# A dynamic convolution and a two-layer feed-forward block: 64-row matmul tiles in pairs, 1024-token superblocks, and one x tile with shifted views

## The chip, the cores and the metric

The kernel runs on one core of a Trainium2 chip. Times are microseconds (us) of device time for one execution. A median is given with its lowest and highest run. A ratio is computed as the mean time of one kernel's fast runs over the mean time of the other's in the same rounds, so it is not quite the ratio of the medians that are quoted; its 95% interval stands in brackets. "Fast" is the undisturbed state of an execution. Runs that were made only once have no known state, and this text says so where it uses one.

Engines in the profile: PE is the tensor engine (PEld its weight loads), DVE the vector engine, ACT the scalar engine, POOL is GpSimd, SP the engine whose queue issues most of the transfers. "L124" is line 124 of the kernel in question.

## The reference

For every token and each of 8 heads, a softmax over 7 weights is taken, and the token's 24 channels of that head become the weighted sum of the token itself and its six predecessors. The result, 192 channels, goes through two matrices with `h - tanh(h)` between them.

```python
# x: (8, 4096, 192); weight_gen: (8, 4096, 8, 7); w_in: (192, 2048); w_out: (2048, 192)
w = np.exp(weight_gen - max);  w = w / (sum(w) + 1e-09)
x_unf = x_pad[:, idx, :]                       # seven shifted copies of x, zeros before the start
conv = np.einsum('bshk,bskhg->bshg', w, x_unf) # (8, 4096, 192)
h = conv.reshape(32768, 192) @ w_in
out = (h - np.tanh(h)) @ w_out                 # (32768, 192)
```

## The kernel before

It works through 64 superblocks of 512 tokens. A partition holds every 128th token, so each of the seven taps is its own load of x (seven times the bytes). GpSimd multiplies each tap by its weights, the vector engine adds the taps in pairs, and PE transposes and adds the four sums by matmuls with the identity. 192 channels are split into 128 and 64, the second part padded to 128 rows.

```python
        for k in range(K):                      # seven loads of x
            xs_k = xpool.tile([P, NB, D], FP32, name=f"xs{k}", tag=f"xs{k}")
            ...
        for k in range(K):
            prod = ppool.tile([P, NB, DP], BF16, name=f"prod{k}", tag=f"prod{k}")
            nc.gpsimd.tensor_mul(
                prod[:, :, 0:D].rearrange("p j (h g) -> p j h g", h=H),
                xs[k][:].rearrange("p j (h g) -> p j h g", h=H),
                wsm[:, :, :, k : k + 1].to_broadcast([P, NB, H, G]),
            )
        ...
                    nc.vector.tensor_add(       # pairs of taps
                        acc[:, :, 0:D], prods[taps[0]][:, :, 0:D], prods[taps[1]][:, :, 0:D]
                    )
        ...
            for g in range(NG):                 # transposition and sum, 4 x 128 columns
                nc.tensor.matmul(
                    pc[:, 0:P], lhsT=gsums[g][:, j0, 0:D0], rhs=ident[:],
                    start=st0, stop=False,
                )
        ...
            nc.tensor.matmul(ph[:, 0:TOK], lhsT=w_in0[:, fa * P : (fa + 1) * P],
                             rhs=convT[:], start=True, stop=False)
            ...
            nc.scalar.activation(out=th[:], in_=ph[:], func=ACT.Tanh)
            nc.vector.tensor_sub(gt[:], ph[:], th[:])
```

(Arguments are folded onto fewer lines here, comments are added, and parts are left out at the "..." lines.) The order of the parts on each engine comes from the framework's scheduler, with pools of two to four buffers deciding what may run ahead.

The softmax here doesn't subtract the row's maximum and nothing guards it: scores larger than these inputs give would overflow.

## Time and profile before

| | before |
|---|---|
| median of 3 runs (lowest to highest) | 1046.02 us (1043.23 to 1046.31) |
| span of the profiled run, granted PE clock | 1041.2 us, 0.987 |
| busy: PE, DVE, ACT, POOL | 89%, 77%, 64%, 71% |
| bytes moved by the DMA queues | 211.48 MB |

The "busy" line of the page gives, for each engine, the microseconds in which it worked, the share of the span, and the number of instructions. A group line gives line, engine, operation and shapes, then busy time and the mean duration in ns of one, then the idle time ahead of them with what ended most of it. A line of the waits reads: engine and line, "<-" what it waited for, then total us, how many times, and the longest. In short: PE is close to its rate through the middle of the kernel, and the other engines have 23% to 36% of their time to spare.

### The profile page before, as it was taken

How to read it: one execution, taken by the hardware profiler on the slowest of the kernel's cores; microseconds unless marked ns; L12 is line 12 of the kernel's file. 1: busy time of each engine (PE TensorE's matmuls, PEld its weight loads, DVE VectorE, ACT ScalarE, POOL GpSimd, SP SyncE). 2: the span in 40 equal slices, each digit the busy share in tenths (PEclk: the TensorE clock that was granted, in tenths of full speed). 3: DMA queues.
4: the chain of work that ended last, by engine and by line, in shares of the span. 5: the costliest groups of instructions: out<-in, count | busy, mean ns of one | idle time of the engine just before them, and what ended most of it. 6: DMA issues, size and time to landing. Idle time of an engine off the chain costs nothing.

```text
span 1041.2 us, 20956 instructions
## 1 busy us (share of the span) xinstructions
PE 931.3 (89%) x8192; PEld 661.6 (64%) x8192; DVE 803.0 (77%) x945; ACT 665.2 (64%) x961; POOL 739.3 (71%) x713
## 2 busy tenths in 40 slices
PE   0576777798999999999999999999999999999998
PEld 0344554465666777667776777667776777777776
DVE  1587777797887888788887888788887888877665
ACT  0254445465666777767776777677776777777775
POOL 4868868898786778867787778867787777882000
PEclk9999899899999999999999999999999999999999
DMA  8947588687997787777776777777876777510001
GB/s 167 314 132 230 169 242 250 202 264 223 331 289 208 236 242 222 220 214 235 238 219 205 236 237 233 216 211 231 243 223 202 235 227 239 153 62 27 21 31 47
DMA packets 306579, 211.48 MB, mean 203 GB/s; under 512 B 44312, under 2 KB 306288, under 8 KB 306480
## 3 DMA queue, kind: packets, MB, share of 16 engines
q1 hardware_dynamic: 304192, 208.58, 67.4%
q0 software_dynamic: 2288, 1.57, 1.1%
q8 instruction: 64, 1.05, 0.4%
q14 instruction: 35, 0.29, 0.1%
HBM read 186.52 MB, written 25.17 MB: 203 GB/s over the span
## 4 chain that ended last, share of the span: by engine, by line
PE 55%; POOL 17%; DVE 9%; issue 5%; ACT 5%; SPq 4%; DMA 3%; POOLq 0%; ACTq 0%; DVEq 0%
POOL prod L155 17%; PE po L272 10%; PE po L279 10%; PE ph L248 8%; PE ph L227 7%; PE ph L234 7%; PE ph L241 7%; DVE gt L258 5%; PE pc L194 2%; DVE gsum L174 2%; DMA wg_t<-in_weight_gen_dram 2%; SPq L123 2%; PE pc L206 2%; PE pc L198 2%; PE pc L202 2%
## 5 line engine op out<-in xcount | busy, mean ns | idle before, releaser
L155 POOL TENSOR_TENSOR prod<-xs,wsm 128x768 bf16<-128x768 f32 x448 | 687.1, 1563 | 100.1 <-DVE wsm L146 45.5
L256 ACT ACTIVATE th<-ph 128x1024 f32<-128x1024 f32 x512 | 519.1, 1023 | 283.9 <-PE ph L248 270.9
L258 DVE TENSOR_TENSOR gt<-ph,th 128x1024 bf16<-128x1024 f32 x512 | 609.9, 1210 | 83.0 <-ACT th L256 82.4
L272 PE MATMUL po<-w_out_t,gt 128*128 128x192 bf16 x2048 | 383.4, 248 | 2.1 <-ACT out_sb L288 2.1
L279 PE MATMUL po<-w_out_t,gt 128*128 128x192 bf16 x2048 | 383.1, 248 | 0.0
L227 PE MATMUL ph<-convT,w_in 128*128 128x512 bf16 x512 | 196.6, 384 | 57.0 <-DVE gt L258 55.5
L279 PEld LDWEIGHTS <-gt 128*128 128x128 bf16 x2048 | 201.8, 99 | 27.2 <-issue 4.8
L272 PEld LDWEIGHTS <-gt 128*128 128x128 bf16 x2048 | 201.9, 99 | 24.7 <-issue 1.3
L248 PE MATMUL ph<-convT,w_in 128*128 128x512 bf16 x512 | 197.1, 385 | 0.0
L241 PE MATMUL ph<-convT,w_in 128*128 128x512 bf16 x512 | 196.8, 384 | 0.0
L234 PE MATMUL ph<-convT,w_in 128*128 128x512 bf16 x512 | 196.6, 384 | 0.0
L174 DVE TENSOR_TENSOR gsum<-prod,prod 128x768 bf16<-128x768 bf16 x192 | 137.1, 759 | 41.1 <-POOL prod L155 41.1
L179 POOL MEMSET gsum<- 128x128 uint32 x192 | 38.6, 204 | 127.9 <-DVE gsum L174 126.5
L194 PE MATMUL pc<-ident,gsum 128*128 128x128 bf16 x384 | 84.9, 221 | 42.9 <-DVE gsum L174 32.1
L234 PEld LDWEIGHTS <-w_in 128*128 128x128 bf16 x512 | 50.4, 98 | 66.0 <-issue 65.8
L241 PEld LDWEIGHTS <-w_in 128*128 128x128 bf16 x512 | 50.5, 99 | 62.0 <-issue 3.0
L198 PE MATMUL pc<-ident,gsum 128*128 128x128 bf16 x384 | 84.9, 221 | 4.0 <-POOL gsum L179 3.9
L206 PE MATMUL pc<-ident,gsum 128*128 128x128 bf16 x384 | 85.1, 222 | 0.0
L248 PEld LDWEIGHTS <-w_in 128*128 128x128 bf16 x512 | 50.5, 99 | 54.4 <-issue 2.2
L202 PE MATMUL pc<-ident,gsum 128*128 128x128 bf16 x384 | 85.1, 222 | 0.0
L194 PEld LDWEIGHTS <-gsum 128*128 128x128 bf16 x384 | 38.0, 99 | 55.8 <-DVE gsum L174 33.2
L198 PEld LDWEIGHTS <-gsum 128*128 128x128 bf16 x384 | 37.8, 98 | 54.2 <-issue 26.3
(31 smaller groups left out, 579.6 us busy)
## 6 DMA issues: line engine op xcount, KB each, us to landing
xs<-in_x_dram SPq DMA_DIRECT2D x400, 384.0 KB
out_dram<-out_sb SPq DMA_DIRECT2D x64, 384.0 KB
xs<-in_x_dram SPq DMA_DIRECT2D x48, 288.0 KB
wg_t<-in_weight_gen_dram SPq DMA_DIRECT2D x64, 112.0 KB
w_out_t<-in_moe_w_out_dram POOLq DMA_DIRECT2D x1, 768.0 KB, 17.0
xs<-in_x_dram SPq DMA_DIRECT2D x8, 95.2 KB
xs<-in_x_dram SPq DMA_DIRECT2D x8, 94.5 KB
xs<-in_x_dram SPq DMA_DIRECT2D x8, 93.8 KB
```

The source lines that it names most:

```text
L155: nc.gpsimd.tensor_mul(prod[:, :, 0:D].rearrange("p j (h g) -> p j h g", h=H), xs[k][:].rearrange("p j (h g) -> p j h g", h=H), wsm[:, :, ...
L174: nc.vector.tensor_add(acc[:, :, 0:D], prods[taps[0]][:, :, 0:D], prods[taps[1]][:, :, 0:D])
L194: nc.tensor.matmul(pc[:, 0:P], lhsT=gsums[g][:, j0, 0:D0], rhs=ident[:], start=st0, stop=False,)
L198: nc.tensor.matmul(pc[:, P : 2 * P], lhsT=gsums[g][:, j1, 0:D0], rhs=ident[:], start=False, stop=False,)
L227: nc.tensor.matmul(ph[:, 0:TOK], lhsT=w_in0[:, fa * P : (fa + 1) * P], rhs=convT[:], start=True, stop=False,)
L234: nc.tensor.matmul(ph[:, TOK : 2 * TOK], lhsT=w_in0[:, fb * P : (fb + 1) * P], rhs=convT[:], start=True, stop=False,)
L241: nc.tensor.matmul(ph[:, 0:TOK], lhsT=w_in1[:, fa * P : (fa + 1) * P], rhs=convT1[:], start=False, stop=True,)
L248: nc.tensor.matmul(ph[:, TOK : 2 * TOK], lhsT=w_in1[:, fb * P : (fb + 1) * P], rhs=convT1[:], start=False, stop=True,)
L256: nc.scalar.activation(out=th[:], in_=ph[:], func=ACT.Tanh)
L258: nc.vector.tensor_sub(gt[:], ph[:], th[:])
L272: nc.tensor.matmul(po[:, 0:D], lhsT=gts[ft // 2][:, gto + j0 * P : gto + (j0 + 1) * P], rhs=w_out_t[:, ft, :], start=(ft == 0), stop=False,)
L279: nc.tensor.matmul(po[:, D : 2 * D], lhsT=gts[ft // 2][:, gto + j1 * P : gto + (j1 + 1) * P], rhs=w_out_t[:, ft, :], start=False, stop=(ft ...
```

## The change

The intent is less work for the tensor engine. 192 channels are three times 64, so in tiles of 64 rows nothing is padded; two 64-row tiles (the upper and the lower half of the array) work at once. In the first matmul and the transposition each works on its own half of the tokens; in the second matmul they take the two halves of the hidden rows, for two successive token blocks. A partition holds eight consecutive tokens plus the six before them, so one x tile of 14 tokens serves all taps as shifted views, and the seven taps are added in PSUM by PE itself, so the vector engine's tap sums and GpSimd's zero fills go. The superblock grows to 1024 tokens. The core of the diff, cut at "...", with arguments folded and comments added:

```diff
-    TOK = 512 if S % 512 == 0 else S
+    J = 8
+    TOK = P * J
 ...
-    xpool = ctx.enter_context(tc.tile_pool(name="xpool", bufs=3))
-    wgpool = ctx.enter_context(tc.tile_pool(name="wgpool", bufs=3))
-    ppool = ctx.enter_context(tc.tile_pool(name="ppool", bufs=3))
+    xpool = ctx.enter_context(tc.tile_pool(name="xpool", bufs=2))
+    wgpool = ctx.enter_context(tc.tile_pool(name="wgpool", bufs=2))
+    ppool = ctx.enter_context(tc.tile_pool(name="ppool", bufs=2))
 ...
+        x_t = xpool.tile([P, HALO + J, D], FP32, name="x_t")
+        lo = 0
+        if s == 0:                      # first superblock of a batch row
+            lo = 1
+            nc.vector.memzero(x_t[0:1, 0:HALO, :])
+            nc.sync.dma_start(out=x_t[0:1, HALO : HALO + J, :], in_=x[b, 0:J]...)
+        ...
+            ap=[[J * D, P - lo], [D, HALO + J], [1, D]],
+        nc.sync.dma_start(out=x_t[lo:P, :, :], in_=src)
 ...
+            nc.gpsimd.tensor_mul(
+                prod[:].rearrange("p c j h g -> p j h c g"),
+                x_t[:, k : k + J, :].rearrange("p j (h c g) -> p j h c g", h=H, c=NC),
+                wsm[:, :, :, k : k + 1]...to_broadcast([P, J, H, NC, GC]),
+            )
 ...
-                    nc.vector.tensor_add(
-                        acc[:, :, 0:D], prods[taps[0]][:, :, 0:D], prods[taps[1]][:, :, 0:D]
-                    )
+        for k in range(K):              # conv(n, chunks): 84 pairs of 64 columns
+            for ci, c in enumerate(chunks):
+                for j in range(JH):
+                    col = (ci * JH + j) * R
+                    for r in range(2):
+                        nc.tensor.matmul(
+                            pc[:, r, col : col + R],
+                            lhsT=prods[k][r * R : (r + 1) * R, c, 2 * j : 2 * j + 2]...,
+                            rhs=ident[r * R : (r + 1) * R, r * R : (r + 1) * R],
 ...
+        for c in range(NC):             # gemm1(n, f): 3 pairs of 512 columns
+            for r in range(2):
+                nc.tensor.matmul(ph[:, r, :],
+                    lhsT=w_in[r * R : (r + 1) * R, c, f * P : (f + 1) * P],
+                    rhs=convT[r * R : (r + 1) * R, c, :],
 ...
+    for r in range(2):                  # w_in once for each half of the array
+        for h in range(H):
+            nc.gpsimd.dma_start(out=w_in[r * R + h * GC : r * R + (h + 1) * GC], ...)
 ...
+    order = tc.manual_schedule(engines={mybir.EngineType.PE})
+    ctx.enter_context(order)
 ...
+    for n in range(NTOT + 1):
+        if n + 2 < NTOT:
+            softmax(n + 2)
+            products(n + 2)
+        if n + 3 < NTOT:
+            load(n + 3)
+        for p in range(J):
+            if n < NTOT:
+                gemm1(n, 2 * p)
+                gemm1(n, 2 * p + 1)
+            if n >= 1:
+                gemm2((n - 1) * J + p)
+            if n + 1 < NTOT:
+                if p == 2:
+                    conv(n + 1, (0, 1))
+                if p == 5:
+                    conv(n + 1, (2,))
```

The order as written is fixed for **PE alone**; where an instruction stands on the other engines is the scheduler's choice.

## The prediction

> **What bounds the kernel now.** I read the page's busy times and groups first, then the timeline of the tensor engine in mid-kernel, then the waits, then the timelines of the vector engine and of GpSimd. The busy line and four groups of the page:
>
> ```profile
> PE 931.3 (89%) x8192; PEld 661.6 (64%) x8192; DVE 803.0 (77%) x945; ACT 665.2 (64%) x961; POOL 739.3 (71%) x713
> ...
> L155 POOL TENSOR_TENSOR prod<-xs,wsm 128x768 bf16<-128x768 f32 x448 | 687.1, 1563 | 100.1 <-DVE wsm L146 45.5
> L256 ACT ACTIVATE th<-ph 128x1024 f32<-128x1024 f32 x512 | 519.1, 1023 | 283.9 <-PE ph L248 270.9
> L258 DVE TENSOR_TENSOR gt<-ph,th 128x1024 bf16<-128x1024 f32 x512 | 609.9, 1210 | 83.0 <-ACT th L256 82.4
> ```
>
> All four engines are busy for most of the span, PE most. Whether PE is at its rate shows in the starts of its matmuls (start, duration, name):
>
> ```profile
> 600.19 0.22 PE L194 MATMUL pc<-ident,gsum 128*128 128x128 bf16 x1
> 600.24 0.22 PE L198 MATMUL pc<-ident,gsum 128*128 128x128 bf16 x1
> ...
> 600.41 0.25 PE L272 MATMUL po<-w_out_t,gt 128*128 128x192 bf16 x1
> 600.49 0.25 PE L279 MATMUL po<-w_out_t,gt 128*128 128x192 bf16 x1
> ...
> 601.07 0.38 PE L227 MATMUL ph<-convT,w_in 128*128 128x512 bf16 x1
> 601.29 0.38 PE L234 MATMUL ph<-convT,w_in 128*128 128x512 bf16 x1
> ```
>
> Start to start is 0.056 us for 128 columns, 0.0825 for 192 and 0.216 for 512; weight loads hide behind them. A 512-token superblock has 32 matmuls of 128 columns, 64 of 192 and 32 of 512: 1.79 + 5.28 + 6.91 = 13.98 us. The same place recurs in the chain of work every 14.27 us, and 64 x 14.27 = 913 of the 1041 us. So in steady state the kernel is bound by the tensor engine, within 2%. The missing 0.29 us is the wait for the single transposition bank (a 512-column matmul followed by 0.51 us instead of 0.216, once per period). The rest, some 128 us, is filling, draining and waits such as these:
>
> ```profile
> DVE wsm L146 <- POOL prod L155: 55.6, 46, 2.7
> PE ph L227 <- DVE gt L258: 55.5, 39, 4.9
> ```
>
> The vector engine has 46 times stopped at the softmax product for GpSimd, for 1.2 us on average, and PE 39 times for the vector engine. That a wait of this kind holds everything behind it shows in the vector engine's timeline:
>
> ```profile
> 555.99 0.22 DVE L117 MEMSET xs<- 4x192 uint32 x1 [1.21 <-POOL prod L155]
> 556.14 1.15 DVE L258 TENSOR_TENSOR gt<-ph,th 128x1024 bf16<-128x1024 f32 x1
> ```
>
> The memset waits 1.21 us for a product, and the subtraction behind it follows only then. GpSimd's own rate, from its timeline:
>
> ```profile
> 653.45 9.05 POOL L155 TENSOR_TENSOR prod<-xs,wsm 128x768 bf16<-128x768 f32 x6 [0.24 <-DVE wsm L146]
> ```
>
> Six products back to back take 9.05 us, so 1.50 us for 768 elements.
>
> **What the Trainium skill says.** "TensorE: Matmul & The Clock Gate", Part 3 (Packing small matmuls), has matmuls in different row groups overlap and start about 4 ns apart; no run here shows it yet. The same page, section "Wait — 56ns, not 53.3ns?", gives about 25 ns as the least start to start of matmuls; the trace's least is 55 ns, at 128 columns. The same page, under "Architectural detail", calls the vector engine's queue strict FIFO; the memset above agrees. "SBUF — State Buffer", section "Who interferes with whom", says that a vector instruction with two SBUF inputs contends with a GpSimd instruction that reads SBUF; that fits the 46 waits of the softmax product, which has two such inputs.
>
> **The change part by part**, per new superblock of 1024 tokens (32 of them).
>
> PE, first matmul: 16 f tiles x 3 chunks x 2 row tiles of 512 columns, two at once: 48 x 0.216 = 10.4 us, against 64 x 0.216 = 13.8 before, since 192 rows no longer cost 256. Second matmul: 16 x 8 pairs of 192 columns, 128 x 0.0825 = 10.6 us, as before. Transposition: 7 taps x 3 x 4 pairs = 84 pairs of 64 columns; I take two times the skill's 25 ns plus a little, 54 ns a pair (estimate): 4.5 us, against 64 x 0.056 = 3.6. PE alone: 25.5 us against 28.5, worth 3 x 32 = 96 us if PE remained the bound.
>
> Others: 16 tanh at 0.904 back to back plus evacuations, some 21 us. Vector engine: 16 subtractions at 1.08 to 1.2, plus softmax 1.7: 20 us; the tap sums (137 us in all) go. GpSimd: 7 products of 1536 elements, twice 1.50: 3.0 each, 21.0 us; its memsets (51 us) go. Loads of x fall from 7 copies to 14/8 of one; the DMA queues were not the bound. By rates alone PE would bind at 25.5.
>
> But the order in which the vector engine stands matters. The built program has, in the third superblock:
>
> ```
> 72 L181 TensorTensor gt12_1896<-ph_1887,th_1894 128x1024 [waits Activation_49]
> 73 L181 TensorTensor gt13_1907<-ph_1898,th_1905 128x1024 [waits Activation_49]
> 74 L110 TensorTensor wsm_3303<-e_t_3297,zr_3301 128x448 [waits Pool_49]
> 75 L181 TensorTensor gt14_1952<-ph_1943,th_1950 128x1024 [waits Activation_49]
> ```
>
> I followed the semaphore values. While superblock n is computed, this product makes the weights of n+5 in one of two buffers, so it waits for the **last** tap product of n+3 on GpSimd. Those products have two buffers too: the first of n+3 waits for the last transposition of n+1, which PE's fixed order puts at p=5 of superblock n. So all seven products, 21 us, lie between p=5 and the vector engine's gt14 of p=7. Nothing of them is hidden but the 4 us until gt13. The same row recurs in every superblock from the second to the 27th. Two stages that should overlap are in a ring: PE to p=5, GpSimd, vector engine, PE.
>
> The ring's period, from the end of the products (0): softmax product to 0.7 (0.39 for 224 elements, so 0.63 for 448); gt14 to 1.9, which frees the PSUM tile for which PE stands at the second f tile of the next superblock. That f tile, cold, ends at 3.3 and the second matmul of p=0, cold, at 5.9: after an idle gap of 4.28 us at 90.16 us the trace shows 512 columns at 0.43 and 192 at 0.16 us for some 2.6 us, and here PE will have stood over 10. Then p=0's remainder and p=1 to 8.6, p=2 to 11.25, the first transposition 56 x 0.054 to 14.25, three more p at 2.65 to 22.2. There the second transposition frees the first product's buffer: 0.35, then 21.0 on GpSimd. **Period 43.6 us**, where PE's own work is 25.5.
>
> Sum. Start: x and 17 weight transfers on GpSimd's queue to about 15 us; products of superblocks 0, 1, 2 to 78; the vector engine's row order holds superblock 0 until then; second transposition of superblock 1 at 81; products of 3 to 103; the next ring, shorter, to 143. Then 25 periods of 43.6: 1090, at 1233. The end without such waits: 21 to p=5, 7 for the remainder, three superblocks at 25.8, one at 21.3, 15 for the last second matmul and store: 142. Together **1375 us**.
>
> **Rivals.** (a) PE binds: if the ring does not hold, about 82 us of filling and draining plus 31 x 26.4, which is 900. For it speaks that every engine's work is under 26 us; against it, that the queue waits in order. (b) The row tiles do not pair fully, so that a pair in the transposition and the second matmul takes 0.1 us: the ring's PE part grows by 56 x 0.046 + 6 x 16 x 0.017 = 4.2 us, and the end too: about 1490. The 512-column part is not touched. (c) GpSimd is slower on outputs in runs of 8 elements: each tenth adds 2.1 us a period, some 60 us in all; or transposition pairs stream at 29 ns, and 1.4 us a period go: 1340.
>
> **Range and chances.** The ring stands in the program, so it is nearly sure; its two large terms, 21.0 and 22, are each uncertain by some 2 us, so the range is 1290 to 1470. Faster by over 2% needs (a), at 0.06; the middle, 0.02; slower 0.92.
>
> **What would show it.** Right: a vector-engine wait for GpSimd's product at the softmax product of some 17 us, about 26 times; PE busy near 60%; products of about 3.0 us, in bursts of seven with equal pauses; 512-column matmuls in pairs, 0.216 us per pair; slow matmuls after each pause. Wrong: no such wait and PE over 90% busy (rival a), or pairs whose members start 0.05 us or more apart (rival b).

## The result, and the profile after

The changed kernel takes **1441.36 us** (median of 4 runs, 1440.06 to 1442.76), against 1044.97 us (1043.23 to 1046.31) for the kernel before. The ratio is 1.3793 [1.3771, 1.3815]: 38% slower. Its profiled run has a span of 1437.9 us at a granted clock of 0.835.

The busy line and three groups of the changed kernel's page:

```profile
PE 837.2 (58%) x16640; PEld 639.2 (44%) x16640; DVE 662.3 (46%) x616; ACT 643.0 (45%) x865; POOL 654.4 (46%) x247
...
L124 POOL TENSOR_TENSOR prod<-x_t,wsm 128x1536 bf16<-128x1536 f32 x224 | 643.1, 2908 | 685.1 <-PE pc L147 613.3
L181 DVE TENSOR_TENSOR gt<-ph,th 128x1024 bf16<-128x1024 f32 x512 | 601.5, 1215 | 219.2 <-ACT th L179 217.7
L170 PE MATMUL ph<-convT,w_in 64*128 64x512 bf16 x3072 | 416.5, 392 | 443.3 <-DVE gt L181 437.7
```

Every engine has less work than before (PE 837 us instead of 931, DVE 662 instead of 803, POOL 654 instead of 739), and none is busy for more than 58% of the span. The time went into waiting, and the groups say in which circle: GpSimd waits for PE's transposition (613 us), PE for the vector engine's subtraction (438 us). The third side is in the waits of the same kernel:

```profile
POOL prod L124 <- PE pc L147: 613.3, 28, 30.6
...
PE ph L170 <- DVE gt L181: 437.7, 41, 25.8
DVE wsm L110 <- POOL prod L124: 352.1, 23, 26.0
...
DVE x_t L83 <- POOL prod L124: 103.2, 7, 15.6
```

The vector engine stops 23 times at the softmax product (L110) for a GpSimd product, 15.3 us on average; before, the corresponding wait was 46 times 1.2 us. At every fourth superblock another instruction takes its place: the memset of a batch row's leading zeros (L83) waits for the same products, 7 times, 14.7 us on average. One stop at L110 in the vector engine's timeline:

```profile
665.50 2.36 DVE L181 TENSOR_TENSOR gt<-ph,th 128x1024 bf16<-128x1024 f32 x2 [1.08 <-ACT th L179]
683.23 0.62 DVE L110 TENSOR_TENSOR wsm<-e_t,zr 128x448 f32<-128x448 f32 x1 [15.38 <-POOL prod L124]
```

The subtraction for which PE waits stands behind L110 in the queue. GpSimd makes its seven products meanwhile, having waited for PE before:

```profile
663.14 20.06 POOL L124 TENSOR_TENSOR prod<-x_t,wsm 128x1536 bf16<-128x1536 f32 x7 [21.67 <-PE pc L147]
```

21.67 us waiting, then 20.06 us working: a ring of two halves that never overlap. The chain of waits shows one whole turn of it (start, duration, what it was; x32 counts matmuls):

```profile
602.32 1.46 PE ph L170 x6
603.78 2.40 PE po L200 x32
606.18 1.29 PE ph L170 x12
607.48 1.32 PE po L200 x32
...
611.41 1.75 PE pc L147 x112
...
621.21 0.83 PE pc L147 x56
...
624.27 17.21 POOL prod L124 x6
...
664.33 35.17 DMA out_dram<-out_sb
```

Three things are to be seen. The same 32 matmuls take 2.40 us just after the pause and 1.32 us later: PE is slow in the first 3.9 us after it (1.46 and 2.40 us; the granted clock was 0.54 there and 1.00 in the 5.8 us that follow). The second transposition at 621 us lets the products run to 641 us. And at the end of this stretch a store of 768 KB took 35.17 us to land, which is a second thing, found below: it comes with every fourth superblock, the first of a batch row.

From the fifth superblock's products on, the first products of successive superblocks start 40.6 to 41.7 us apart three times in a row, and then once 50.0 to 50.7 us apart (the very last pair is 23.8 us apart). The mean of the 25 turns that the prediction counted is 43.4 us.

The start of GpSimd's work, from its timeline, and the line of the window from 60 to 75 us (busy time of PE, PEld, DVE, ACT, POOL, then clock, DMA share and GB/s):

```profile
74.62 17.58 POOL L124 TENSOR_TENSOR prod<-x_t,wsm 128x1536 bf16<-128x1536 f32 x6 [41.18 <-DMA x_t<-in_x_dram]
```

```profile
60.00:75.00 15.00, 0.00 (x0) 0.00 (x0) 0.00 (x0) 0.00 (x0) 0.38 (x1) 1.00 0.06 24
```

The first product starts at 74.6 us, because x is not there. During that wait the DMA engines are at a share of 0.06, which is one of sixteen, and move 24 GB/s. The load of a batch row's first superblock covers partitions 1 to 127 (partition 0 begins with zeros and has its own small load): 1333.5 KB, some 57 us at that rate. At the row head of the chain above, one took 55 us: it was issued at 641.8 us, and its last packet ended at 696.6 us.

### The profile page after: what moved, and what is told of

The parts are those of the page before. It is cut to its first block, busy times and chain, and to the rows that moved or that the text cites. A ratio compares the mean times of both kernels' runs of the same rounds, so it can differ in the third digit from the quotient of the medians.

```text
span 1437.9 us, 36105 instructions
## 1 busy us (share of the span) xinstructions
PE 837.2 (58%) x16640; PEld 639.2 (44%) x16640; DVE 662.3 (46%) x616; ACT 643.0 (45%) x865; POOL 654.4 (46%) x247
## 4 chain that ended last, share of the span: by engine, by line
PE 38%; POOL 30%; DMA 14%; DVE 6%; another core or an unknown queue 5%; issue 5%; ACT 1%; POOLq 0%; DVEq 0%; ACTq 0%
POOL prod L124 30%; PE po L200 18%; PE ph L170 15%; DMA out_dram<-out_sb 12%; PE pc L147 5%; DVE gt L181 4%; DMA w_in<-in_moe_w_in_dram 2%; DVE wsm L110 1%; ACT th L179 1%; DVE x_t L83 0%; ACT out_sb L225 0%; DVE zsum L104 0%; ACT e_t L98 0%; POOLq L124 0%
## 5 line engine op out<-in xcount | busy, mean ns | idle before, releaser
L124 POOL TENSOR_TENSOR prod<-x_t,wsm 128x1536 bf16<-128x1536 f32 x224 | 643.1, 2908 | 685.1 <-PE pc L147 613.3
L170 PE MATMUL ph<-convT,w_in 64*128 64x512 bf16 x3072 | 416.5, 392 | 443.3 <-DVE gt L181 437.7
L200 PE MATMUL po<-w_out,gt 64*128 64x192 bf16 x8192 | 419.5, 255 | 48.9 <-ACT out_sb L225 47.9
L200 PEld LDWEIGHTS <-gt 64*128 64x128 bf16 x8192 | 388.1, 100 | 111.7 <-issue 64.1
L170 PEld LDWEIGHTS <-w_in 64*128 64x128 bf16 x3072 | 165.4, 96 | 576.3 <-issue 485.7
L110 DVE TENSOR_TENSOR wsm<-e_t,zr 128x448 f32<-128x448 f32 x32 | 25.3, 792 | 352.1 <-POOL prod L124 352.1
L147 PE MATMUL pc<-ident,prod 64*128 64x64 bf16 x5376 | 101.8, 198 | 104.0 <-POOL prod L124 91.5
L147 PEld LDWEIGHTS <-prod 64*128 64x128 bf16 x5376 | 98.5, 100 | 105.9 <-POOL prod L124 92.4
L225 ACT ACTIVATE out_sb<-po 128x192 f32<-128x192 f32 x256 | 85.0, 332 | 117.0 <-PE po L200 64.7
L157 ACT ACTIVATE convT<-pc 128x1024 bf16<-128x1024 f32 x64 | 51.7, 810 | 63.6 <-PE pc L147 63.6
L83 DVE MEMSET x_t<- 1x1152 uint32 x8 | 8.1, 1018 | 104.3 <-POOL prod L124 103.2
## 6 DMA issues: line engine op xcount, KB each, us to landing
x_t<-in_x_dram SPq DMA_DIRECT2D x8, 1333.5 KB
```

The source lines that it names most:

```text
L110: nc.vector.tensor_mul(wsm[:].rearrange("p j h k -> p (j h) k"), e_t[:].rearrange("p j h k -> p (j h) k"), zr[:].rearrange("p (n o) -> p n ...
L124: nc.gpsimd.tensor_mul(prod[:].rearrange("p c j h g -> p j h c g"), x_t[:, k : k + J, :].rearrange("p j (h c g) -> p j h c g", h=H, c=NC), ...
L147: nc.tensor.matmul(pc[:, r, col : col + R], lhsT=prods[k][r * R : (r + 1) * R, c, 2 * j : 2 * j + 2].rearrange("p j h g -> p (j h g)"), rh ...
L157: nc.scalar.activation(out=convT[:, c0 : c0 + nch, :].rearrange("p c (j r t) -> p r (c j) t", r=2, t=R), in_=pc[:, :, 0 : nch * JH * R].re ...
L170: nc.tensor.matmul(ph[:, r, :], lhsT=w_in[r * R : (r + 1) * R, c, f * P : (f + 1) * P], rhs=convT[r * R : (r + 1) * R, c, :], start=(c == ...
L200: mm = nc.tensor.matmul(po[:, 0:D], lhsT=g_of[n][f][r * R : (r + 1) * R, col : col + P], rhs=w_out[r * R : (r + 1) * R, f, :], start=(r == ...
```

## The experiments

Two theories at first. **The ring**: the place of the softmax product in the vector engine's queue makes GpSimd's products and PE's work take turns. The rival is that GpSimd, or PE with its smaller tiles, is simply too slow. A second question was what the 127-partition load costs. All kernels gave correct results. Medians of the kernel before in the same rounds lay between 1044.77 and 1046.19 us.

| run | median us (lowest to highest) | ratio to before |
|---|---|---|
| changed kernel | 1441.36 (1440.06 to 1442.76) | 1.3793 [1.3771, 1.3815] |
| e1_order | 1107.56 (1107.05 to 1109.92) | 1.0603 [1.0587, 1.0619] |
| e2_split | 1326.34 (1326.11 to 1327.36) | 1.2694 [1.2675, 1.2713] |
| e3_both | 903.76 (903.28 to 904.01) | 0.8648 [0.8634, 0.8662] |
| e4_pool2, e5_prod3, e6_wg4 | 1904.38, 1460.61, 1407.09 (one look each, state unknown) | none |
| e7_full2 | 921.71 (921.55 to 923.12) | 0.8812 [0.8791, 0.8833] |
| e8_mid | 887.03 (884.67 to 888.34) | 0.8470 [0.8444, 0.8497] |
| e9_start | 867.11 (865.21 to 867.53) | 0.8290 [0.8271, 0.8309] |
| e10_spread | 875.96 (875.18 to 877.55) | 0.8375 [0.8357, 0.8394] |
| e11_early | 885.52 (878.28 to 888.87) | 0.8456 [0.8407, 0.8506] |
| e12_fewer | 870.45 (868.22 to 871.28) | 0.8317 [0.8300, 0.8333] |

### e1_order: the order as written on the vector and scalar engines too

```diff
-    order = tc.manual_schedule(engines={mybir.EngineType.PE})
+    order = tc.manual_schedule(
+        engines={mybir.EngineType.PE, mybir.EngineType.DVE, mybir.EngineType.Activation}
+    )
```

> Edit: the vector engine and the scalar engine keep the program's order too, not the tensor engine alone; nothing else. Theory ring (the softmax product of superblock n+5 stands in the vector engine's queue ahead of subtractions of superblock n and waits for products that PE's fifth step releases): that product now stands at the start of superblock n for n+2 and waits for products long done, so no wait of over 4 us at it, the period falls from 43.5 to about 25 us where loads arrive in time, PE's clock rises from 0.83 to over 0.95. At batch starts the load of x into 127 partitions, which took over 50 us, then comes late: some 15 us at each of 7. Time 980 to 1050 us. Rival PE (row tiles themselves set the period): 1441 us, unchanged. Rival products (GpSimd's 20.1 us is the bound, with waits around it): period not below 40 us.

Measured: 1107.56 us, 334 us less than the changed kernel. No computation was altered and no buffer added. From the third batch row on, the first products are 25.1 to 26.2 us apart within a row, and 50.5 to 50.8 us apart from one row to the next. The vector engine's wait for a product at the softmax product is gone from the waits; what leads GpSimd's waits instead is the load:

```profile
POOL prod L124 <- DMA x_t<-in_x_dram: 261.0, 8, 41.4
```

Eight waits for eight batch rows. So the ring is the scheduler's order, not the speed of an engine. The edit fixes two engines at once; that the vector engine's order is what counts is read from this wait, not from a run that fixes that engine alone. The expected time was missed: the load costs about 25 us at each row, where some 15 had been assumed, and PE's clock rose to 0.92 instead of over 0.95.

### e2_split: the 127-partition load in two, partitions 1 to 15 and 16 to 127

```diff
+        if lo:
+            q = 16
+            nc.sync.dma_start(
+                out=x_t[lo:q, :, :],
+                in_=bass.AP(tensor=win.tensor, offset=win.offset,
+                            ap=[[J * D, q - lo], [D, HALO + J], [1, D]]),
+            )
+            src = bass.AP(tensor=win.tensor, offset=win.offset + (q - lo) * J * D,
+                          ap=[[J * D, P - q], [D, HALO + J], [1, D]])
+            lo = q
         nc.sync.dma_start(out=x_t[lo:P, :, :], in_=src)
```

> Edit: at a batch start, the load of x into partitions 1 to 127 is issued as two, 1 to 15 and 16 to 127; order as in the changed kernel. Theory transfer: the one for 127 partitions runs on a sixteenth of the DMA engines, 1333.5 KB at some 24 GB/s; it kept the first products until 74.6 us and adds 10 us to every fourth period through a store queued behind it. With the split the first products start at about 34 us, when the weight transfers are issued, and all ring periods are 40 to 42: 1441 - 41 - 7 x 10 = 1330 us. Rival bandwidth (weights and loads share the bandwidth): no change over 10 us. The ring stays in both: softmax product waits of over 13 us remain.

Measured: 1326.34 us, as expected; 115 us less than the changed kernel. The first product starts at 27.1 us instead of 74.6, and every turn of the ring takes 40.6 to 42.2 us; the turns of 50 us are gone. The ring itself stays, as its wait shows:

```profile
DVE wsm L120 <- POOL prod L134: 336.9, 22, 17.0
```

So the load explains the slow start and the fourth turn, and nothing of the other three.

### e3_both: both edits together

The diff is the two above, unaltered: the order fixed on three engines, and the load cut at partition 16.

> Edit: both of the above. Ring and transfer theories together: first products at 34 us, superblock 0 ended at 88, then 31 x 24.5 us and 13 us at the end: 860 us, faster than the kernel before by some 18%. If the row tiles did not pair in a dense stream, periods would be 28 us and more: over 960. If GpSimd bound: 20.1 us, lower than PE's 23.5, so not.

Measured: **903.76 us**, 13.5% faster than the kernel before. The busy line of its page, and two of its DMA issues (KB of each, median us from issue to landing):

```profile
PE 780.9 (87%) x16640; PEld 600.2 (67%) x16640; DVE 675.4 (75%) x616; ACT 643.2 (71%) x865; POOL 653.4 (72%) x247
```

```profile
x_t<-in_x_dram SPq DMA_DIRECT2D x24, 1344.0 KB, 5.7
...
x_t<-in_x_dram SPq DMA_DIRECT2D x8, 1176.0 KB, 6.8
```

128 partitions (1344 KB) land in 5.7 us and 112 partitions (1176 KB) in 6.8 us, where 127 partitions (1333.5 KB) took 55. The Trainium skill has the reason, on its page "DMA: Bandwidth & Descriptors", section "Why a DMA increments its semaphore by 16 and not by 1": a transfer is spread over the largest number of engines, up to 16, that divides its outer dimension, and 127 partitions are its example for one engine. The trace agrees: share 0.06 for 127, and about a tenth of the time for 128. The prediction had not looked this up. The store that landed after 35 us was in flight together with such a load, and with the load split the slow fourth turns are gone. The packets in the trace of the changed kernel show why: 120 of the store's 128 packets had moved by 671 us; the last eight, its share on the one busy engine, moved from 697.2 to 699.0 us, after the load's last packet had ended at 696.6.

The expected 860 us were missed by 44. The period is 25.2 us, in which PE streams for 23.4: 48 x 0.216 + 128 x 0.0825 + 84 x 0.0293 = 10.4 + 10.6 + 2.5. Most of the rest is one wait for a subtraction that stands behind the softmax, 1.4 us long. The start also lost time. Superblock 1 begins at 87 us, as foretold, but superblock 0 had kept PE for 38.1 us and superblock 1 takes 31.0. In superblock 0 PE stands 17.0 us for a subtraction behind this softmax product:

```profile
51.88 15.89 DVE L120 TENSOR_TENSOR wsm<-e_t,zr 128x448 f32<-128x448 f32 x1
```

It takes 0.62 us elsewhere. Here GpSimd was making products from 27.20 to 67.29 us, and the softmax product ended only after that, at 67.77. Both of its inputs lie in SBUF, which is the case of contention that the prediction cites.

### e4_pool2: every product made twice

```diff
-            nc.gpsimd.tensor_mul(
+            for _ in range(2):
+                nc.gpsimd.tensor_mul(
```

> Edit: in the changed kernel each tap product on GpSimd is written twice, so that GpSimd has 40.2 us of work per superblock instead of 20.1; the result stays right. Theory ring: GpSimd's seven products lie in the ring at full length, so each of some 24 ring periods grows by 20 us, and the first three superblocks and the last by 20 too: 1441 + 28 x 20 = 2000 us. Rival overlap (GpSimd is beside PE, which sets the period of 43.5): 40.2 still fits beside 43.5 and the time changes by under 5%.

Measured: 1904.38 us in one look, state unknown, far beyond a few per cent of any run's scatter. The 2000 us expected were missed by 96. GpSimd's timeline has the doubled products and a wait for PE before them:

```profile
892.04 40.20 POOL L125 TENSOR_TENSOR prod<-x_t,wsm 128x1536 bf16<-128x1536 f32 x14 [16.56 <-PE pc L148]
```

The turns take 56.8 to 59.2 us, about 58.1 on average, which is 40.2 plus 17.9. If products and PE overlapped, 40.2 us of GpSimd would still have fitted beside the 43.5, and the period would have stayed. So the rival, overlap, falls. No turn stands out at the row heads any more; the late store may be hidden in the longer turn. Against an undisturbed turn of the changed kernel, 41.1 us on average, it is 17.0 longer: 20.1 more for the products, 3 less for PE's part. The test is not a clean one: with the longer products the scheduler put the softmax product behind the second subtraction of a superblock instead of the fourteenth (the order of the trace shows it), which probably lets a little more of PE's work go beside the products.

### e5_prod3 and e6_wg4: more buffers, the scheduler's order kept

```diff
-    ppool = ctx.enter_context(tc.tile_pool(name="ppool", bufs=2))
+    ppool = ctx.enter_context(tc.tile_pool(name="ppool", bufs=3))
```

> Edit: in the changed kernel the products on GpSimd have three buffers instead of two; nothing else. Theory ring by order: the built order runs one superblock further ahead, and the softmax product of n+6 stands at the same place (after the 14th subtraction of superblock n) and waits for the products of n+4, whose buffer the same transposition of superblock n's fifth step releases; so the ring stays, with a period of 43 to 44 us: 1441 us within 2%. Rival buffers (a third buffer uncouples GpSimd from PE): period 25 to 35 us, time under 1250.

```diff
-    wgpool = ctx.enter_context(tc.tile_pool(name="wgpool", bufs=2))
+    wgpool = ctx.enter_context(tc.tile_pool(name="wgpool", bufs=4))
```

> Edit: in the changed kernel the softmax tiles have four buffers instead of two; nothing else. Theory ring by order: in the built order the softmax product of n+7 takes the place of that of n+5 and waits for the products of n+3, released by the same transposition; period 43 to 44 us, 1441 us within 2%. Rival buffers (the write-after-read on two softmax buffers is the cause): the wait goes, under 1250 us.

Measured, in one look each: 1460.61 and 1407.09 us, the second a little outside the 2% that was expected. In both, nearly all turns stay at 40.6 to 50.8 us. The built programs show why: with more buffers the scheduler puts the softmax product further ahead (one superblock with three product buffers, two with four weight buffers), so that it waits for the products being made at that moment, as before; the order and the waits of 15.4 us in the traces agree. The 34 us that e6 gained are at the end: its last three turns take 24 to 25 us, where the changed kernel has one such turn. Why e5 lost 19 us was not followed. More buffers do not open this ring, because the order on the queue follows the buffers.

### e7_full2: e3 with the second matmul in 128-row tiles

```diff
         for f in range(NFT):
-            for r, n, j, po in ops:
-                ...
-                    lhsT=g_of[n][f][r * R : (r + 1) * R, col : col + P],
-                    rhs=w_out[r * R : (r + 1) * R, f, :],
+            nc.tensor.matmul(
+                po[:, 0:D],
+                lhsT=g_of[n][f][:, col : col + P],
+                rhs=w_out[:, f, :],
+                start=(f == 0),
+                stop=(f == NFT - 1),
+            )
```

> Edit, on the kernel with the order kept and the transfer split (904 us): the second matmul in 128-row tiles as in the kernel before, first matmul and transpositions in pairs of 64 rows as they are; result unchanged. By streaming alone 16 matmuls of 192 columns take the same 1.32 us as 16 pairs: 904 us within 1%. Theory drain ([...]the tile mode changes, 16 times per superblock): if each change costs 0.1 to 0.3 us, 1.6 to 4.8 us per period: 950 to 1050 us.

Measured: 921.71 us, 18 us more than e3. Arithmetic is the same: one 128-row matmul of 192 columns takes the 0.0825 us that a pair of 64-row ones took. What is added is the change between the two shapes of tile. From the last 512-column matmul to the first 192-column one it is 0.308 us from start to start, where the second of a pair in e3 is followed after 0.196; back again 0.178 instead of 0.0825. So each change costs about 0.1 us, 16 times in a superblock, 1.6 us, of which 0.9 shows in the period (26.1 us instead of 25.2). The expectation named two outcomes and the truth lies between them. Here the small row tiles of the second matmul gain nothing by themselves; they save the changes.

### e8_mid: softmax and products in the middle of a superblock

```diff
-            nc.vector.memzero(x_t[0:1, 0:HALO, :])
+            nc.gpsimd.memzero(x_t[0:1, 0:HALO, :])
 ...
-        if n + 2 < NTOT:
-            softmax(n + 2)
-            products(n + 2)
 ...
                 if p == 2:
                     conv(n + 1, (0, 1))
+                    if n + 2 < NTOT:
+                        softmax(n + 2)
+                        products(n + 2)
```

> Edit, on the kernel with the order kept and the transfer split (904 us): softmax and products of n+2 are issued after the first transposition of n+1 (third step) instead of at the start of superblock n, and the zeros of a batch's first rows are written by GpSimd. The period there is 25.2 us, of which PE's streams are 23.5 (10.4 + 10.6 + 2.5); at the superblock's start the vector engine does 1.8 us of softmax while PE waits for the subtractions behind it. Theory softmax bubble: beside the transposition, which needs no subtraction, it is hidden: period 23.7 to 24.4, time 904 - 31 x 1.1 = 870 us. Rival (vector and scalar engine set the period at 25.2 by their own work, some 20 us, and latencies): no change over 1%.

Measured: 887.03 us, 17 us less than e3. The gain is in the start and in the turns of 26 to 28 us at the head of a batch row, which are gone. By e3's chain of work these turns belong to the edit's second part: the memset of the zeros, 1.02 us, stood between the softmax and the subtraction for which PE waited, and now it is GpSimd's. The period stayed at 25.2 us, so the step that was to bring it to 24 failed.

### e9_start: e8 with half of the weight loads replaced by a copy within SBUF

```diff
-    for r in range(2):
-        for h in range(H):
-            nc.gpsimd.dma_start(
-                out=w_in[r * R + h * GC : r * R + (h + 1) * GC],
+    for h in range(H):
+        nc.gpsimd.dma_start(
+            out=w_in[h * GC : (h + 1) * GC],
 ...
+    nc.sync.dma_start(out=w_in[R:P], in_=w_in[0:R])
 ...
                 if p == 2:
-                    conv(n + 1, (0, 1))
+                    if n > 0:
+                        conv(n + 1, (0, 1))
 ...
-                if p == 5:
+                if p == 5 and n == 0:
+                    conv(1, (0, 1))
+                if p == (5 if n > 0 else 7):
                     conv(n + 1, (2,))
```

> Edit, on the kernel of 887 us (softmax in mid superblock): the second copy of the first weights is made by one transfer within SBUF instead of eight more transfers issued by GpSimd, so that GpSimd issues 9 instead of 17 and none waits for another; the transpositions of superblock 1 are issued at the fifth and seventh step of superblock 0 instead of the second and fifth. There the first products started at 30.6 us and superblock 1 at about 74. Theory start: products start at 10 to 14 us, all behind them moves forward by some 15 to 20 us, period unchanged at 25.2: 865 to 875 us. Rival (x itself lands only at 25 us or later, or the weights come too late): no change over 5 us.

Measured: **867.11 us**, as expected, and the lowest median: 17% faster than the kernel before. Nine weight issues on GpSimd instead of seventeen let the first product start at 12.2 us instead of 30.6. Why the period is still 25.2 us is in its chain of waits:

```profile
450.70 1.65 PE pc L157 x112
...
453.29 0.58 ACT e_t L108
...
453.89 0.63 DVE zsum L114
...
454.55 0.56 DVE zr L118
...
455.20 0.62 DVE wsm L120
455.83 1.15 DVE gt L191
...
457.02 0.82 PE ph L180 x6
```

Exponential, sum, reciprocal and product follow each other on two engines, and the subtraction that PE needs stands behind them. PE pauses for 1.6 us here in every period, at the same place of each superblock, and for 0.2 us after the second transposition: 23.4 + 1.8 = 25.2.

### e10_spread: one softmax part per step

```diff
+            if n + 2 < NTOT and p < 4:
+                softmax_part(n + 2, p)      # exp, sum, reciprocal, product
+                if p == 3:
+                    products(n + 2)
```

> Edit, on e9_start: the four softmax operations of n+2 are issued one by one behind the first four steps of superblock n (exponential, sum, reciprocal, product), and the products after the fourth. In the kernel before it the chain of waits showed them end to end after the transposition, 2.4 us in which PE stood: that is why its period stayed at 25.2. Theory bubble: one at a time each fits in the slack of a step (2.64 us of PE against some 2.36 of subtractions), period 24.0 to 24.6, 31 x 0.9 = 28 us less than e9_start. Rival (the three PSUM tiles shared with the transpositions set the period): 25.2 stays and the time is that of e9_start within 5 us.

Measured: 875.96 us, 9 us more than e9: a miss. The pause behind the softmax is gone, but the products now begin a step later, and the last tap is not ready when the transposition comes to it:

```profile
433.83 0.41 PE L173 MATMUL pc<-ident,prod 64*128 64x64 bf16 x16 [1.65 <-POOL prod L150]
```

Those 16 matmuls are the seventh tap, after 96 of the other six. The wait is 1.57 us in most periods, and the period is 25.6 us.

### e11_early: the same parts, two steps earlier

```diff
+            if n + 2 < NTOT and (p < 2 or n == 0 and p < 4):
+                softmax_part(n + 2, p if n == 0 else p + 2)
+                if p == (3 if n == 0 else 1):
+                    products(n + 2)
+            if n + 3 < NTOT and p >= 6:
+                softmax_part(n + 3, p - 6)
```

> Edit, on e10_spread: the four softmax operations stand two steps earlier on and the last two of them two steps earlier still (exponential and sum of n+3 behind the last two steps of superblock n, reciprocal and product behind the first two of the next), so the products on GpSimd start two steps sooner. In e10_spread PE waited 36 times for the products, 72 us in all, as they were put off to the fourth step: 20.1 us from there end behind the third step of the next superblock. Theory products late: that wait goes, the period falls from 25.6 to 24.0 to 24.4, the time to 830 to 840 us. Rival (PSUM tiles or evacuation set it): period 25.2 or more, 863 us or more.

Measured: 885.52 us, and a wide scatter (878.28 to 888.87): a miss again. Some periods are 24.0 us, as hoped. But others take up to 30.5, and PE now pauses in a new way:

```profile
409.49 1.36 PE L173 MATMUL pc<-ident,prod 64*128 64x64 bf16 x81
413.17 0.62 PE L173 MATMUL pc<-ident,prod 64*128 64x64 bf16 x31 [2.32 <-issue]
```

"issue" says that no semaphore was waited for. After the first 100 us there are 21 pauses of 1.1 to 4.4 us, 48.4 us in all. Counting PE's matmuls from the first, every one of the 21 stands at the same remainder, 93, modulo 128 (of 128, not of the 512 of which the next expectation speaks); with the weight load of each, 128 matmuls are 256 instructions. The Trainium skill, "Runtime: NRT & Kernel Launch", section "Instruction fetch mechanics", has instructions fetched in blocks of 256 and calls the cost of crossing a block "mostly hidden". The trace agrees on the block: the instruction queue brings 130 packets of 16 KB for PE's 16640 matmuls and as many weight loads, 256 instructions for each packet. The length of the pauses differs from what the page says. In the pause shown, such a packet moves from 410.96 to 411.93 us, after the x load and the store had kept the DMA engines at a share of 0.93 from 404 to 410 us, and PE goes on at 413.17. It is so in all 21: each ends 1.2 to 1.5 us after the end of such a packet. So the new theory was that PE, no longer pausing elsewhere, runs out of instructions.

### e12_fewer: e11 with a quarter fewer PE instructions

The second matmul goes to 128-row tiles, as in e7: 392 matmuls in a superblock instead of 520. If arithmetic were the bound, the changes of tile shape would make this slower, as they did in e7.

```diff
         for f in range(NFT):
-            for r, n, j, po in ops:
-                ...
-                    lhsT=g_of[n][f][r * R : (r + 1) * R, col : col + P],
+            nc.tensor.matmul(
+                po[:, 0:D],
+                lhsT=g_of[n][f][:, col : col + P],
```

> Edit, on e11_early: the second matmul in 128-row tiles, as in e7_full2, so that PE has 392 matmuls per superblock instead of 520. In e11_early many periods are 24.0 us, as foretold, but 21 times PE stops for 1.1 to 4.4 us without a semaphore, each time before the 93rd matmul of a block of 512, that is at a fixed count of instructions, beside a late packet of the instruction queue. Theory instructions (PE runs through its stream faster than the packets come, when loads and stores fill the DMA engines): with a quarter fewer the pauses are at most 5; each period costs up to 1.6 us for the changes of tile mode, so 24.8 to 25.6, and the time is 845 to 875 us. Rival (the pauses have another cause, tied to the schedule): about as many pauses, time over 885 us.

Measured: 870.45 us, **15 us less than e11**, where the same edit had cost 18 us between e3 and e7. Six pauses over 0.8 us are left, 8.4 us in all, and all six again stand at that same remainder modulo 128. Most periods are 25.0 to 25.2 us, and the chain of waits in mid-kernel is PE alone, one piece after the other:

```profile
508.59 1.43 PE po L221 x16
510.02 1.74 PE pc L173 x112
511.76 1.29 PE ph L196 x12
513.05 1.43 PE po L221 x16
514.48 1.40 PE ph L196 x12
```

This supports the shortage of instructions; it was not tested by moving the loads, so what delays the instruction packets, the transfers of x or something else, stays open. e12 ends level with e9 (the intervals of their ratios overlap): e9 pauses for the softmax, e12 pays for the tile changes.

## Why the prediction was right, and where its sum was off

The direction, the mechanism and the range were right. The ring was read out of the built program before a run, and it is what the traces show. The steps, one by one:

| step, as the prediction put it | predicted, ends at us | measured, ends at us | difference so far |
|---|---|---|---|
| products of superblocks 0, 1, 2 | 78 | 135.9 | +58 |
| products of 3 | 103 | 161.4 | +58 |
| next ring, "shorter" | 143 | 212.0 | +69 |
| 25 periods | 1233 | 1296.4 | +63 |
| the end | 1375 | 1437.9 (span) | +63 |

**The start** is the term that was mis-sized: "x and 17 weight transfers on GpSimd's queue to about 15 us" measured 74.6. The load of partitions 1 to 127 ran on one DMA engine, and the prediction counted "Loads of x fall from 7 copies to 14/8 of one" by bytes only. e2 shows it by splitting that load alone. The 11 us that the next ring adds are a row head, of which below. The weight issues on GpSimd come next: with x early, e2 still starts at 27.1, and e9, with nine issues instead of seventeen, at 12.2.

**The period** of 43.6 was met by a mean of 43.4, but that is luck: two errors cancel in it. Nineteen of the 25 turns average 41.1 us, 2.5 less than predicted; six average 50.5, so each row head adds 9.4. The missing 2.5 us are GpSimd's seven products (20.1 instead of 21.0) and PE's part (21.1 instead of 22.55 from the end of the products to the next first product), of which the transposition is 1.3: 112 matmuls took 1.75 and 1.63 us, 29 to 31 ns a pair, where the prediction had taken 54. The surplus at the row heads is the store whose last packets stand behind the 127-partition load, which the prediction had not foreseen. e2 shows all turns at 40.6 to 42.2.

**The vector engine's wait** at the softmax product was expected as "some 17 us, about 26 times" and was 15.3 us, 23 times. That its row recurs in every superblock was not quite so: at row heads the memset takes that place. PE busy "near 60%" was 58%. Products of "about 3.0 us" were 2.87 within a burst (20.06 / 7). Slow matmuls after each pause are there, 2.40 us against 1.32.

**Rival (a)**, PE as the bound at about 900 us, did not come in this kernel, but it is what e3 became, at 903.76, when the scheduler's order and the load were put right. That the two numbers meet is partly luck: the period is 25.2 us instead of 26.4, and the start and the end take longer than the 82 us assumed. PE's own work was 23.4 us a superblock against 25.5 foretold. The gain foretold for PE mixes two things: the 28.5 us of before hold the wait of 0.29 us for every 512 tokens; by the prediction's own streams it is 28.0, so 2.5 x 32 = 80 us and not 96. **Rival (b)**, pairs that do not stream, fell: 32 matmuls of 192 columns take 1.32 us (0.0825 a pair) and 6 of 512 take 0.65 us (0.216 a pair). **Rival (c)** had one half right: the transposition pairs do stream at 29 ns. Its other half fell: outputs in runs of eight elements did not slow GpSimd, at 2.87 us for 1536 elements against 1.50 for 768 before.

On the skill's four places: the strict order of the vector engine's queue carries the whole result, and every run here agrees. The contention between the vector engine and GpSimd was not tested by a run, but the traces agree with it. The softmax product, with both inputs in SBUF, takes 0.62 us, but up to 3.3 us in the changed kernel, 15.9 in e3 and 20.5 in e2 when GpSimd is making products; in the kernel before, the 39 tap sums that lay beside products for over half of their time took 1.88 us in the median, those beside none 0.55. The subtraction, with one input in PSUM, takes 1.22 us in both cases. The prediction's example was the wrong one: its 46 waits end with a semaphore of GpSimd, and are no contention. The two figures for matmul starts are in the last section.

What stays open is what delays the instruction packets, and what e9 would gain if the softmax pause and the fetch pauses could both be avoided.

## What to carry to other kernels

Before trusting a gain in one engine's work, look in the built program where each instruction stands in its queue, and follow the semaphore of every one that waits for a slower engine: an instruction placed too far ahead can put two stages into turns, and more buffers then only move it further ahead. Check the partition count of every large transfer; 127 instead of 128 cost 55 us against 6. And when a pause has been removed, expect the next one beneath it: here 334 us came from the order alone, 115 from the load alone (204 once the order was right), and the last 37 from two small steps (e8, e9), while two more (e10, e11) failed because each uncovered another wait.

## What the Trainium skill lacked or had wrong

- "TensorE: Matmul & The Clock Gate", section "Wait — 56ns, not 53.3ns?": about 25 ns as the least start to start of matmuls. In two row tiles, 112 matmuls of 64 columns took 1.63 us, 14.6 ns each on average, so the floor does not hold across row tiles (a pair took 29 ns).
- The same page, Part 3: starts about 4 ns apart within a pack. The trace of the changed kernel has the two of a pair 15 to 20 ns apart, and the next pair about 200 (512 columns), 65 (192) or 14 ns (64) after that. The span of a pair still equals one matmul, so the conclusion stands.
- "Runtime: NRT & Kernel Launch", section "Instruction fetch mechanics": crossing a block is called mostly hidden. In e11, 21 pauses of 1.1 to 4.4 us stand at one place of the 256-instruction blocks, 48.4 us in all; e12, with a quarter fewer PE instructions, has six, 8.4 us. That this is the fetch is supported by e12 and by the instruction packets that end 1.2 to 1.5 us before PE goes on; why they come late is not shown.
- The change from 64-row to 128-row tiles and back has no time on any page (it belongs to "TensorEngine Tiling (Array Packing)"): about 0.1 us each in e7 (0.308 instead of 0.196 us, and 0.178 instead of 0.0825).
- The page "DMA: Bandwidth & Descriptors" was right on 127 partitions; the runs add the figures: 24 GB/s and 55 us, against 5.7 us for 1344 KB on 128 partitions.
- "SBUF — State Buffer", section "Who interferes with whom", gives no length for the contention of a vector instruction with a burst of GpSimd instructions: 0.62 us became up to 3.3 us in the changed kernel, 15.9 in e3 and 20.5 in e2.
